# Slot sums kept in SBUF, eight turning PSUM banks, and one row load of a unit cut into 24 and 8 rows, in an attention and soft-MoE kernel on one core

## The chip, the core and the metric

The kernel runs on one core of a Trainium2 chip. The metric is the device time of one execution in microseconds (us). Executions of one kernel lie within a few per cent of each other (the kernel before: 180.0 to 186.27 us over all batches, 3.5%). A run that is over 1.5% above the fastest run of the same kernel counts as "slow". A profile comes from one execution, so a single figure from one profile carries the noise of one run.

## The reference

The kernel computes attention with 8 heads over 8 batches of 576 tokens, and feeds the result to a soft mixture of experts.

```python
# q, k, v: (8 batches, 8 heads, 576 tokens, 64), float32
scores = (q @ k.transpose(0, 1, 3, 2)) / 8
# heads 0-3: the last 32 tokens; heads 4-7: every 4th of the last 128
scores = where(mask[head], scores, -1e6)
x = softmax(scores) @ v                      # -> (4608 tokens, 512)

logits = x @ phi                             # (4608, 32): 8 experts x 4 slots
d = softmax over tokens(logits)
slot_input = d.T @ x                         # (32, 512): the "slot sums"
slot_out[e] = relu(slot_input[e] @ w1[e]) @ w2[e]   # w1: 512x1024, w2: 1024x512
out = softmax over slots(logits) @ slot_out  # (4608, 512)
```

## The kernel before

A Python scheduler places every operation on the five engines before the kernel is built: each operation has a key and a modelled length, and PSUM banks and SBUF rings come from pools. A different pool or key therefore moves instructions on every engine.

The work is cut into eight units (two batches of one head type). Three staging buffers hold the inputs of three units. All loads are issued by one queue, in a fixed order: u0, u1, u2, w10, u3, w11, u4, w12, u5, w13, u6, w14, u7, w15, w16, w17, p3a, p0, p1, p2, p3b. The names w1x are halves of the experts' first layers, p0 to p3b are parts of the second layers. A unit's q, k and v go to 32 partitions each, weights go to 128 partitions, and all are cast from float32 to bfloat16 on the way (the page before has 61.93 MB read from HBM and 30.94 MB on the load queue).

```python
def load_unit(u):
    bp, ty, s = u // 2, u % 2, u % 3
    def f(g):
        for t, src in enumerate((q, k, v)):
            dst = stg[32 * t:32 * t + 32, s, :]
            two = src[2 * bp:2 * bp + 2]
            if ty == 0:
                ...                                   # two loads of 18 KB rows
            else:                                     # one load: 32 rows of 36 KB
                g.dma_start(dst, two[:, 4:8].rearrange("b h (p c) d -> (h p) b (c d)", c=2 * CT))
```

The kernel uses eight PSUM banks. Bank 7 holds the slot sums for the whole kernel, and the other seven turn:

```python
psA  = ps[:, 7, :]
psum = Pool(7, {1: [[6]] + one[:6], 2: [[0, 1], [2, 3], [4, 5]]})
...
i_ = t.matmul(psA[32 * g:32 * g + 32, 256 * ty:256 * ty + 256], et, xb,
              start=b == 0 and i < 4, stop=b == B - 1)         # slot sums, batch b
```

The tail runs after the last batch: slot sums, first layer, then the second layer's matmuls in the order in which its weights arrive (p3a, p0, p1, p2, p3b). The row sum of the output's softmax ("rsum", 36 matmuls) is placed after p1's matmuls. so_sb is the scaled second-layer output; from it the 9.4 MB of output are computed and stored.

```python
PARTS = [("p3a", 3, 0, 8), ("p0", 0, 0, 16), ("p1", 1, 0, 16), ("p2", 2, 0, 16), ("p3b", 3, 8, 16)]
...                            # per part and half: matmuls that need that part's weights
op("pe", rsum, r=b_expT + [b_rowm], w=[rs], alloc=[rs], cost=1.5, key=K1 + 3, after=[mid])
```

The scheduler also has fillers: matmuls whose result nobody reads. They are put where its model leaves a gap of over 0.4 us on TensorE, inside a window FILL of model time. They are meant to keep TensorE's clock up; every kernel here has some of them, so no run shows whether they do.

```python
FILL = (125, 148)
if e == "pe" and fill[0] < t0 and free[e] < fill[1]:
    gap = t0 - max(free[e], fill[0])
    n = min(int((gap - 0.15) / 0.216), 64)
    ...                                             # n filler matmuls, 128x512 each
```

The softmax here doesn't subtract the row's maximum and nothing guards it: scores larger than these inputs give would overflow.

## Time and profile before

The kernel took 181.75 us (median of 3 runs, 180.95 to 182.5).

| what | before |
|---|---|
| span of the profiled execution | 178.9 us |
| load queue (q0), share of all 16 DMA engines' span | 82.9% |
| last weight load, p3b: its sixteen parts land | 147.60 to 151.81 us |
| row sum ends | 151.98 us |
| so_sb starts | 153.24 us |

The landings are the times of the sixteen increments that the load's semaphore gets. I read each as the part of one of the sixteen DMA engines. These come from the trace's semaphore records.

First the page of the kernel before: PEclk is the granted TensorE clock in tenths of full speed and GB/s the load and store rate, each in 40 slices of the span; the last line is a DMA queue with its packets, megabytes and share.

```profile
span 178.9 us, 5741 instructions
...
PEclk9999999999699999999999999999999999999655
...
GB/s 77 198 235 224 187 214 210 228 223 198 221 208 212 243 216 194 213 212 214 236 202 211 214 214 218 233 216 209 227 216 209 216 196 68 78 420 439 469 469 235
...
q0 software_dynamic: 3600, 30.94, 82.9%
```

Counting slices from 0, loads run at some 215 GB/s without a break until slice 32, and before the output the clock is down in slice 10 only. Next the chain that ended last, for the same kernel: start in us, length in us, what ran. "issue" is time in which TensorE (PE) waited for nothing that the profile shows. L849 is the row sum, L834 the second layer's matmuls.

```profile
42.31 1.82 issue
...
64.04 1.05 issue
...
77.21 1.12 issue
...
102.97 1.08 issue
...
150.01 1.97 PE ps L849 x36
151.98 1.24 PE ps L834 x40
153.24 0.49 DVE so_sb L860
```

The row sum ends just after p3b has landed, matmuls of p2 and p3b follow in 1.24 us, and so_sb can start. The loads and the compute chain end together.

### The profile page before, as it was taken

How to read it: one execution, taken by the hardware profiler on the slowest of the kernel's cores; microseconds unless marked ns; L12 is line 12 of the kernel's file. 1: busy time of each engine (PE TensorE's matmuls, PEld its weight loads, DVE VectorE, ACT ScalarE, POOL GpSimd, SP SyncE). 2: the span in 40 equal slices, each digit the busy share in tenths (PEclk: the TensorE clock that was granted, in tenths of full speed). 3: DMA queues.
4: the chain of work that ended last, by engine and by line, in shares of the span. 5: the costliest groups of instructions: out<-in, count | busy, mean ns of one | idle time of the engine just before them, and what ended most of it. 6: DMA issues, size and time to landing. Idle time of an engine off the chain costs nothing.

```text
span 178.9 us, 5741 instructions
## 1 busy us (share of the span) xinstructions
PE 131.7 (74%) x2602; PEld 99.8 (56%) x2602; DVE 116.6 (65%) x262; ACT 92.1 (52%) x132; POOL 27.8 (16%) x56
## 2 busy tenths in 40 slices
PE   0019768885997977978898879788699999889000
PEld 0019557674775955756886757586565569432000
DVE  6980596994279569668859947969974020799200
ACT  2005957843574886568589557477331100599000
POOL 7960402500400250230020010010200000000000
PEclk9999999999699999999999999999999999999655
DMA  5999899999999999999999999999999993299995
GB/s 77 198 235 224 187 214 210 228 223 198 221 208 212 243 216 194 213 212 214 236 202 211 214 214 218 233 216 209 227 216 209 216 196 68 78 420 439 469 469 235
DMA packets 5015, 40.79 MB, mean 228 GB/s; under 512 B 1408, under 2 KB 1408, under 8 KB 1792
## 3 DMA queue, kind: packets, MB, share of 16 engines
q0 software_dynamic: 3600, 30.94, 82.9%
q1 hardware_dynamic: 1392, 9.50, 12.7%
q8 instruction: 20, 0.33, 0.7%
q14 instruction: 3, 0.02, 0.0%
HBM read 61.93 MB, written 9.44 MB: 399 GB/s over the span
## 4 chain that ended last, share of the span: by engine, by line
PE 44%; DVE 32%; ACT 6%; DMA 5%; issue 5%; POOL 1%; DVEq 0%; POOLq 0%
DVE XB L634 9%; DVE PT L584 9%; PE ps L532 7%; PE ps L678 5%; DVE WD L907 5%; DVE VN L599 5%; DMA stg<-in_v_dram 5%; PE ps L651 4%; PE ps L527 4%; PE ps L594 4%; PE ps L924 3%; ACT PT L576 3%; PE ps L569 3%; PE ps L623 2%; PE ps L787 2%
## 5 line engine op out<-in xcount | busy, mean ns | idle before, releaser
L551 ACT ACTIVATE TT<-ps 128x864 f32<-128x864 f32 x32 | 28.6, 896 | 32.9 <-PE ps L532 24.0
L576 ACT ACTIVATE PT<-ps 128x768 bf16<-128x768 f32 x48 | 36.7, 812 | 8.9 <-PE ps L569 8.8
L532 PE MATMUL ps<-ident,stg 96*64 96x96 bf16 x576 | 18.0, 224 | 18.3 <-DMA stg<-in_v_dram 12.8
L634 DVE TENSOR_TENSOR XB<-ps,RV 96x768 bf16<-96x768 f32 x32 | 30.3, 947 | 0.6
L532 PEld LDWEIGHTS ps<-ident,stg 96*64 96x64 bf16 x576 | 15.7, 123 | 20.0 <-DMA stg<-in_v_dram 12.8
L599 DVE COPY VN<-ps 128x768 bf16<-128x768 bf16 x32 | 17.5, 546 | 8.8 <-PE ps L594 8.6
L663 DVE COPY XT<-ps 128x576 bf16<-128x576 bf16 x19 | 11.4, 598 | 13.3 <-PE ps L651 13.2
L623 PE MATMUL ps<-VN,PT 128*128 128x65 bf16 x384 | 17.6, 194 | 1.9 <-DVE PT L584 0.9
L569 PE MATMUL ps<-TT 64*128 64x96 bf16 x384 | 15.1, 204 | 4.2 <-issue 1.1
L594 PE MATMUL ps<-ident,TT 128*128 128x128 bf16 x192 | 16.1, 221 | 1.6 <-issue 1.0
L623 PEld LDWEIGHTS ps<-VN,PT 128*128 128x128 bf16 x384 | 14.4, 98 | 4.0 <-DVE PT L584 1.3
L651 PE MATMUL ps<-ident,XB 96*128 96x96 bf16 x192 | 13.1, 209 | 4.4 <-DVE XB L634 4.3
L527 PE MATMUL ps<-ident,stg 96*128 96x96 bf16 x288 | 14.9, 206 | 0.1
L569 PEld LDWEIGHTS ps<-TT 64*128 64x128 bf16 x384 | 9.5, 94 | 7.9 <-ACT PT L576 1.4
L594 PEld LDWEIGHTS ps<-ident,TT 128*128 128x128 bf16 x192 | 10.9, 98 | 5.4 <-issue 2.4
L651 PEld LDWEIGHTS ps<-ident,XB 96*128 96x128 bf16 x192 | 9.8, 99 | 7.0 <-DVE XB L634 6.0
L584 DVE TENSOR_TENSOR PT<-PT,mask_d 128x768 bf16<-128x768 bf16 x24 | 12.9, 546 | 0.5 <-ACT PT L576 0.2
L527 PEld LDWEIGHTS ps<-ident,stg 96*128 96x128 bf16 x288 | 13.0, 98 | 0.3 <-ACT PT L576 0.3
L584 DVE TENSOR_TENSOR PT<-PT,mask_p 128x768 bf16<-128x768 bf16 x24 | 12.6, 538 | 0.0
L894 PE MATMUL ps<-so_sb,expT 128*128 128x512 bf16 x35 | 10.4, 397 | 0.7 <-DVE stg L907 0.2
L664 ACT ACTIVATE XT<-ps 128x576 bf16<-128x576 bf16 x13 | 8.4, 650 | 3.8 <-PE ps L651 3.5
L678 PE MATMUL ps<-XT,phi_pad 128*128 128x192 bf16 (+1 forms) x64 | 10.2, 306 | 0.2 <-ACT XT L664 0.2
(83 smaller groups left out, 162.6 us busy)
## 6 DMA issues: line engine op xcount, KB each, us to landing
WD<-in_moe_w_dram POOLq DMA_DIRECT2D x7, 1024.0 KB, 27.5
stg<-in_moe_w_dram POOLq DMA_DIRECT2D x2, 2048.0 KB, 19.1
out_dram<-WD SPq DMA_DIRECT2D x1, 4096.0 KB, 11.9
stg<-in_q_dram POOLq DMA_DIRECT2D x8, 288.0 KB, 14.9
stg<-in_k_dram POOLq DMA_DIRECT2D x8, 288.0 KB, 16.7
stg<-in_v_dram POOLq DMA_DIRECT2D x8, 288.0 KB, 18.7
stg<-in_q_dram POOLq DMA_DIRECT2D x4, 576.0 KB, 17.9
stg<-in_k_dram POOLq DMA_DIRECT2D x4, 576.0 KB, 19.8
```

The source lines that it names most:

```text
L527: i_ = t.transpose(bankb2(pt, a)[:, 96 * kk:96 * kk + 96], two[:, c, :], ident[0:96, 0:96])
L532: i_ = t.transpose(bankb2(pt, a)[64 * hx:64 * hx + 64, 96 * kk:96 * kk + 96], src[:, hx, c, :], ident[0:96, 0:96])
L551: return ac.activation(d, sv, ACTF.Copy)
L569: i_ = t.matmul(pair(sc)[:, hx, QB * x:QB * x + QB], win(u, 1, h01, blk_, bpar)[64 * hx:64 * hx + 64], win(u, 0, h01, blk_, bpar)[64 * hx: ...
L576: op("act", lambda ac: ac.activation(sbt(pt)[:, 0:768].rearrange("p (x n) -> p x n", x=2), pair(sc)[:, :, 0:384], ACTF.Exp, scale=SCALE), ...
L584: return dv.tensor_tensor(p_, p_, m.unsqueeze(1).to_broadcast([128, 2, 384]), AluOp.mult)
L594: i_ = t.transpose(bankb(pv)[:, 128 * m:128 * m + 128], win(u, 2, h01, m, bpar), ident[:, :])
L599: op("dve", lambda dv: dv.tensor_copy(sbt(vn)[:, :, :, 0:64], bankb(pv)[:, 0:768].rearrange("p (m x d) -> p m x d", m=6, x=2)), r=[pv], w= ...
L623: i_ = t.matmul(pair(po)[:, bk, 65 * po_:65 * po_ + 65], sbt(pts[i])[:, o_:o_ + 128], sbt(vn)[:, m, half, 0:65], start=True, stop=True)
L634: op("dve", lambda dv: dv.tensor_tensor(sbt(xb)[:].rearrange("p m (x h d) -> p h x m d", x=2, h=2)[:, h01], pv()[:, :, :, 0:64], sbt(rv)[: ...
L651: i_ = t.transpose(bankb(px)[:, QB * m:QB * m + QB], sbt(xb)[:, m, 128 * x:128 * x + 128], ident[0:QB, 0:QB])
L678: i_ = t.matmul(o_, phi_pad[:, c].rearrange("p j i -> p (j i)"), rhs, start=c == 0, stop=c == 3)
```

## The change

The intent: give the eighth PSUM bank to the turning pool, by adding the slot sums of two batches at a time into SBUF; let the scheduler make a tighter order with the new pool; even out the sixteen DMA engines by cutting one load; and start the fillers earlier.

```diff
-FILL = (125, 148)
+FILL = (116, 148)
...
+    scr = sb("scr", [8, 64])
...
-    psA = ps[:, 7, :]
-    one = [[i] for i in range(7)]
-    psum = Pool(7, {1: [[6]] + one[:6], 2: [[0, 1], [2, 3], [4, 5]]})
+    psum = Pool(8, {1: [[i] for i in (6, 7, 0, 1, 2, 3, 4, 5)], 2: [[0, 1], [2, 3], [4, 5], [6, 7]]})
...
-    PACE = 13.1
+    SKEW = 5
+    PACE = 10.87
...                                                  # load_unit, 36 KB rows
-                    res.append(g.dma_start(
-                        dst, two[:, 4:8].rearrange("b h (p c) d -> (h p) b (c d)", c=2 * CT)))
+                    rows = two[:, 4:8].rearrange("b h (p c) d -> (h p) b (c d)", c=2 * CT)
+                    if (u, t) != (SKEW, 0):
+                        res.append(g.dma_start(dst, rows))
+                        continue
+                    res.append(g.dma_start(dst[0:24], rows[0:12]))
+                    res.append(g.dma_start(scr[0:8, :], rows[12:16, :, 0:64]))
+                    res.append(g.dma_start(dst[24:32], rows[12:16]))
...                                                  # seven lines of keys, like this one
-           key=due(u, 0.5 * j))
+           key=due(u, 0.57 * j))
...                                                  # slot sums
-                i_ = t.matmul(psA[32 * g:32 * g + 32, 256 * ty:256 * ty + 256],
+                i_ = t.matmul(bank(acc)[32 * g:32 * g + 32, 256 * ty:256 * ty + 256],
...
+        if b == 1:
+            op("dve", lambda dv: dv.tensor_copy(psA_sb[:], bank(acc)), r=[acc], w=[b_psA], ...)
+        elif b % 2:
+            op("dve", lambda dv: dv.tensor_tensor(psA_sb[:], bank(acc), psA_sb[:], AluOp.add), ...)
...
-    op("dve", lambda vv: vv.tensor_copy(psA_sb[:], psA), r=[b_acc], w=[b_psA], cost=0.65, key=K1)
```

The split concerns one of the 24 q, k and v loads, that of q in unit 5. The tiny load of 1 KB goes to a place that nobody reads. With the new order the scheduler puts 33 fillers between the row sum and p2's matmuls and 8 more before p3b's. The order before has none there. I call these 41 the late fillers.

More of the change, by code (lines that the diff above doesn't have):

```diff
@@ L192, in schedule @@
                 got, tal, ok, taken = [], 0.0, True, {}
+                if any(t.phys is None and t not in o.alloc for t in o.touch):
+                    continue
                 for t in o.alloc:
@@ L378, in bass_dilated_sliding_attn__then__soft_moe_slots_kernel @@
     b_id0, b_id, b_sel, b_fold, b_rowm, b_phist, b_phi = [Buf() for _ in range(7)]
-    b_acc, b_psA, b_csum, b_rcs, b_rtok = [Buf() for _ in range(5)]
+    b_psA, b_csum, b_rcs, b_rtok = [Buf() for _ in range(4)]
     b_expT, b_expX = [Buf() for _ in range(B)], Buf()
@@ L402, in f @@
                 else:
-                    res.append(g.dma_start(
-                        dst, two[:, 4:8].rearrange("b h (p c) d -> (h p) b (c d)", c=2 * CT)))
+                    rows = two[:, 4:8].rearrange("b h (p c) d -> (h p) b (c d)", c=2 * CT)
+                    if (u, t) != (SKEW, 0):
+                        res.append(g.dma_start(dst, rows))
+                        continue
+                    res.append(g.dma_start(dst[0:24], rows[0:12]))
+                    res.append(g.dma_start(scr[0:8, :], rows[12:16, :, 0:64]))
+                    res.append(g.dma_start(dst[24:32], rows[12:16]))
             return res
@@ L503, in bass_dilated_sliding_attn__then__soft_moe_slots_kernel @@
     U = [dict() for _ in range(NU)]
-    XB, XT, ET = {}, {}, {}
+    XB, XT, ET, ACC = {}, {}, {}, {}
     def win(u, t, h01, i, bpar):
@@ L552, in st_T @@
         op("act", ev, r=[pt], **{"w" if j == 0 else "a": [b_TT[u % 2]]}, cost=0.8,
-           key=due(u, 0.8 + 0.5 * j))
+           key=due(u, 0.8 + 0.57 * j))
     def bankb2(t, a):
@@ L573, in pe @@
             return i_
-        k0 = due(u, 4.0 + 1.3 * i)
-        op("pe", pe, r=[b_TT[u % 2]], w=[sc], alloc=[sc, pt], cost=0.22, mode="r", key=k0)
+        k0 = due(u, 5.2 + 1.13 * i)
+        op("pe", pe, r=[b_TT[u % 2]], w=[sc], alloc=[sc, pt], cost=0.28, mode="r", key=k0)
         op("act", lambda ac: ac.activation(
@@ L596, in pe @@
             return i_
-        k0 = due(u, 4.5 + 2.0 * g)
+        k0 = due(u, 3.6 + 2.0 * g)
         op("pe", pe, r=[b_id, b_TT[u % 2]], w=[pv], alloc=[pv, vn], cost=0.35, key=k0)
@@ L626, in pe @@
             return i_
-        k0 = due(u, 8.5 + 2.0 * g)
+        k0 = due(u, 6.7 + 2.46 * g)
         op("pe", pe, r=list(pts.values()) + [vn], w=[po], alloc=al, cost=0.46, key=k0)
@@ L653, in pe @@
             return i_
-        k0 = due(u, 13.0 + 4.0 * bpar + 0.8 * x)
+        k0 = due(u, 19.2 + 4.0 * bpar + 0.1 * x)
         op("pe", pe, r=[b_id, xb], w=[px], alloc=al, cost=0.31, key=k0)
@@ L680, in pe @@
             return i_
-        k0 = due(u, 15.5 + 4.0 * (b % 2))
+        k0 = due(u, 17.4 + 4.0 * (b % 2))
         op("pe", pe, r=[x0, x1, b_phi], w=[lg], alloc=[lg], cost=1.0, key=k0)
@@ L716, in st_L @@
         xb0, xb1 = XB[b, 0], XB[b, 1]
+        if b % 2 == 0:
+            ACC[b // 2] = tile(psum, 1)
+        acc = ACC[b // 2]
         def pe3(t):
@@ L721, in pe3 @@
                 g = (m + 2 * ty) % 4
-                i_ = t.matmul(psA[32 * g:32 * g + 32, 256 * ty:256 * ty + 256],
+                i_ = t.matmul(bank(acc)[32 * g:32 * g + 32, 256 * ty:256 * ty + 256],
                               sbt(et)[:, i, :], sbt((xb0, xb1)[ty])[:, m, :],
-                              start=b == 0 and i < 4, stop=b == B - 1,
+                              start=b % 2 == 0 and i < 4, stop=b % 2 == 1 and i % 6 >= 2,
                               skip_group_check=True)
             return i_
-        op("pe", pe3, r=[et, xb0, xb1], a=[b_acc], cost=0.35, mode="c", key=k0 + 4.0)
+        op("pe", pe3, r=[et, xb0, xb1], after=list(acc.ready), a=[acc],
+           alloc=[acc] if b % 2 == 0 else [], cost=0.44, mode="c", key=k0 + 4.0)
+        if b == 1:
+            op("dve", lambda dv: dv.tensor_copy(psA_sb[:], bank(acc)), r=[acc], w=[b_psA],
+               cost=0.6, key=k0 + 4.6)
+        elif b % 2:
+            op("dve", lambda dv: dv.tensor_tensor(psA_sb[:], bank(acc), psA_sb[:], AluOp.add),
+               r=[acc], w=[b_psA], cost=0.6, key=k0 + 4.6)
     W_AFTER = {2: ["w10"], 3: ["w11"], 4: ["w12"], 5: ["w13"], 6: ["w14"],
```

## The prediction

> **What bounds the kernel now.** The DMA bounds the first 150 of 178.9 us: in the page's slices it stays at 9 tenths; the load queue takes 82.9% of all 16 engines' span. The loads are issued in one order and never starve. In the semaphore records of the last weight load, p3b, the sixteen engines' parts land between 147.6 and 151.8 us: eight engines by 148.9, the other eight from 150.1. The compute chain has been tuned to end with it: in the timeline the row-sum matmuls (L849) end at 151.98, 48 small matmuls follow (L834), so_sb starts at 153.24, and from there 25 us of output (9.4 MB) follow, which the change doesn't touch. Both must move: the last load, and the row sum.
>
> **What the change does.**
> 1. An eighth PSUM bank turns (four pairs, not three), against four adds or copies of about 0.69 us on DVE (the length of the old copy, L763), off the end.
> 2. A new order. Replaying both instruction orders with the median length of each operation in this trace, without stalls, I estimate that the row sum ends 6.4 us earlier (139.4 for 145.8).
> 3. The split row load. [...] If the right four are relieved, the slowest engine gains up to 1.2 us; the mean of the last landings is 149.4, so never over 2.4. The least sure step.
> 4. Fillers. The changed order has 33 filler matmuls before p2's matmuls and 8 before p3b's, the old one none. They run, early or late: 41 x 0.216 us = 8.9 us (three took 0.81). They cost nothing only if the row sum ends by about 142.
>
> **Is it early enough?** The trace's row sum ends 6.2 us later than my stall-free replay of the same kernel. The timeline shows why: PE stands still for no visible cause ("issue") at 42.3, 64.0, 71.4, 77.2 and 103 us for 0.5 to 1.8 us, each ending some 1.4 us after a 16 KB packet of the instruction queue; after the longest the granted clock is 0.5 for 3.4 us. [...] A faster PE runs into this more. With like stalls I estimate the row sum at 144 to 147, the fillers then end after p3b has landed, and so_sb starts at 154 to 157: later than now. With few stalls it starts at 151 to 152.4.
>
> **Prediction.** 183.8 us, 179.6 to 188.0 eight times in ten. Faster by over 2% 0.05 (the load floor forbids it), within 2% 0.57, slower by over 2% 0.38.
>
> **What would show it.** Right: row sum ends before 148; the 33 fillers end after p2 (146) and delay p3b's matmuls past its landing; instruction-queue packets ahead of PE gaps; last output still 25 us after so_sb. Wrong: the fillers end before the loads, the chain of waits shows DMA into TT, p3b's slowest part lands near 150.5; then about 180. Slower still if stalls of over 1.5 us bring the half clock twice.

In point 3, that the split relieves four of the sixteen engines is my assumption, and the 1.2 us are my estimate from it: no record of these traces names the engine of a packet.

## The result, and the profile after

The changed kernel took 196.45 us (median of 4 runs, 194.96 to 199.07), against 181.65 us (180.95 to 182.5, 4 runs) for the kernel before on the same chip. The ratio is 1.0785 with a 95% interval of 1.0701 to 1.087: slower. A ratio here is the mean time of one kernel's fast runs over that of the other's fast runs of the same rounds, so it is not quite the ratio of the medians. The time lies far above the predicted range.

| what | before | after |
|---|---|---|
| span of the profiled execution | 178.9 us | 193.3 us |
| p3b: first, mean and last of sixteen landings | 147.60, 149.33, 151.81 | 151.52, 155.82, 157.99 |
| row sum ends | 151.98 | 157.28 |
| late fillers end | none | 167.25 |
| so_sb starts | 153.24 | 167.64 |

The page after, with the same lines as before:

```profile
span 193.3 us, 5830 instructions
...
PEclk9999999988999969999985699995799999999755
...
GB/s 88 208 221 230 189 215 234 212 199 218 213 212 238 179 150 176 187 189 189 190 193 167 214 217 219 222 217 217 217 217 212 185 58 2 0 328 452 414 434 326
...
q0 software_dynamic: 3696, 30.94, 80.8%
```

The same 30.94 MB are loaded, but the rate is down from slice 13 to slice 21 (about 63 to 106 us), to 150 GB/s at the lowest. The clock is down in several stretches and not in one. At the end of the loads there is a hole: slices 33 and 34 move 2 and 0 GB/s, so almost nothing was loaded or stored for some 10 us. The chain that ended last, after (L865 is the row sum, L940 a filler, L850 the second layer):

```profile
38.52 2.93 issue
...
65.68 2.74 issue
...
81.75 1.44 issue
...
89.43 1.44 issue
...
96.53 1.76 issue
...
103.92 2.58 issue
...
155.32 1.97 PE ps L865 x36
...
157.36 7.07 PE ps L940 x32
164.43 0.99 PE ps L850 x32
...
165.58 1.67 PE ps L940 x7
167.25 0.36 PE ps L850 x8
167.64 0.49 DVE so_sb L876
```

Two things are to be seen. The stretches of "issue" are longer: the six shown add up to 12.9 us, the four longest of before to 5.1 us. And the tail has fillers in it: TensorE runs 7.07 us of fillers after the row sum, then p2's matmuls, then 1.67 us of fillers, then p3b's, which had landed at 157.99, long before. The output part has not changed: so_sb starts 14.40 us later, and the span is 14.4 us longer.

The third view is the table of windows: us, busy time with instruction counts of PE, PEld, DVE, ACT and POOL, granted clock, DMA share and GB/s. First before, then after.

```profile
70.00:80.00 10.00, 7.84 (x172) 6.42 (x170) 7.26 (x16) 6.02 (x9) 2.61 (x5) 1.00 1.04 216
...
100.00:110.00 10.00, 8.57 (x186) 6.78 (x188) 6.85 (x15) 5.76 (x11) 0.53 (x1) 1.00 1.03 215
```

```profile
70.00:80.00 10.00, 9.02 (x175) 7.40 (x171) 6.71 (x16) 7.46 (x12) 2.61 (x5) 0.88 1.05 166
...
100.00:110.00 10.00, 6.47 (x116) 5.88 (x116) 2.91 (x5) 3.95 (x6) 0.53 (x1) 0.50 1.01 188
```

From 70 to 80 us, TensorE does about the same number of matmuls, but the DMA moves 166 GB/s for 216, while its share of busy time is the same or higher (1.05 for 1.04). So the engines are not starved of requests; they take longer for each byte. From 100 to 110 us the load rate is still down, and TensorE, at half clock, does 116 matmuls for 186.

The packets' durations say the same. In the second table, "long" is the share of load packets in a stretch of 3 us that took over 5% more than the usual time of their size (for instance 1378 ns for 18 KB and 625 ns for 8 KB).

```
packets of 18,432 B, us       median   nine in ten below
before, 60 to 110 us          1.378    1.378
after, 60 to 85 us            1.378    1.983
after, 85 to 110 us           1.525    1.880

after, at us                  60     63     69    75    81     90    99     from 105 on
share of long packets         0.03   0.55   1.0   1.0   0.19   1.0   0.78   0.01
```

### The profile page after: what moved, and what is told of

It is laid out like the page before. It is cut to its first block, busy times and chain, and to the rows that moved or that the text cites. A ratio compares the mean times of both kernels' runs of the same rounds, so it can differ in the third digit from the quotient of the medians.

```text
span 193.3 us, 5830 instructions
## 1 busy us (share of the span) xinstructions
PE 144.0 (74%) x2635; PEld 109.3 (57%) x2642; DVE 111.0 (57%) x253; ACT 97.9 (51%) x144; POOL 29.0 (15%) x58
## 3 DMA queue, kind: packets, MB, share of 16 engines
q0 software_dynamic: 3696, 30.94, 80.8%
## 4 chain that ended last, share of the span: by engine, by line
PE 53%; DVE 13%; ACT 12%; issue 9%; DMA 5%; POOL 1%; DVEq 0%; POOLq 0%
PE ps L539 10%; PE ps L940 7%; ACT PT L583 7%; PE ps L534 6%; PE ps L685 5%; PE ps L630 5%; DVE WD L923 5%; DMA stg<-in_v_dram 5%; PE ps L601 4%; PE ps L658 3%; PE ps L576 3%; DVE XB L641 2%; PE ps L850 2%; DVE PT L591 2%; PE ps L803 2%
## 5 line engine op out<-in xcount | busy, mean ns | idle before, releaser
L539 PE MATMUL ps<-ident,stg 96*64 96x96 bf16 x576 | 18.9, 238 | 21.3 <-DMA stg<-in_v_dram 12.7
L539 PEld LDWEIGHTS ps<-ident,stg 96*64 96x64 bf16 x576 | 17.5, 134 | 22.3 <-DMA stg<-in_v_dram 12.7
L671 ACT ACTIVATE XT<-ps 128x576 bf16<-128x576 bf16 x25 | 15.8, 661 | 9.1 <-PE ps L658 9.1
L601 PE MATMUL ps<-ident,TT 128*128 128x128 bf16 x192 | 17.6, 231 | 1.1 <-ACT TT L558 1.0
L639 DVE RECIPROCAL RV<-ps 96x12 f32<-96x12 f32 x32 | 7.0, 220 | 19.9 <-PE ps L630 19.7
L576 PE MATMUL ps<-TT 64*128 64x96 bf16 x384 | 16.1, 207 | 1.6 <-ACT expT L690 1.0
L534 PE MATMUL ps<-ident,stg 96*128 96x96 bf16 x288 | 14.8, 206 | 1.4 <-issue 1.4
L940 PE MATMUL ps<-mask_p,ident 128*128 128x512 bf16 x59 | 14.8, 388 | 0.8 <-issue 0.7
L658 PE MATMUL ps<-ident,XB 96*128 96x96 bf16 x192 | 14.8, 229 | 0.3 <-DVE XB L641 0.3
L601 PEld LDWEIGHTS ps<-ident,TT 128*128 128x128 bf16 x192 | 12.2, 104 | 3.5 <-ACT TT L558 1.4
L658 PEld LDWEIGHTS ps<-ident,XB 96*128 96x128 bf16 x192 | 11.7, 112 | 1.1 <-DVE XB L641 0.4
```

Of the source, the lines that this page charges most:

```text
L534: i_ = t.transpose(bankb2(pt, a)[:, 96 * kk:96 * kk + 96], two[:, c, :], ident[0:96, 0:96])
L539: i_ = t.transpose(bankb2(pt, a)[64 * hx:64 * hx + 64, 96 * kk:96 * kk + 96], src[:, hx, c, :], ident[0:96, 0:96])
L576: i_ = t.matmul(pair(sc)[:, hx, QB * x:QB * x + QB], win(u, 1, h01, blk_, bpar)[64 * hx:64 * hx + 64], win(u, 0, h01, blk_, bpar)[64 * hx: ...
L601: i_ = t.transpose(bankb(pv)[:, 128 * m:128 * m + 128], win(u, 2, h01, m, bpar), ident[:, :])
L658: i_ = t.transpose(bankb(px)[:, QB * m:QB * m + QB], sbt(xb)[:, m, 128 * x:128 * x + 128], ident[0:QB, 0:QB])
L940: i_ = te.matmul(bank(t)[:, 0:512], ident[:, :], mask[0][:].rearrange("p m x -> p (m x)")[:, 0:512], start=True, stop=True)
```

## The experiments

My first theory was this. The split slows the loads; later loads, and with them a later fetch of instructions, make the row sum late; a late row sum exposes the fillers. The rival: the new order by itself makes TensorE stall more, so that the row sum would be late, and the fillers exposed, without the split too. Eleven runs were made, of ten kernels (a_neither was run twice), in three batches, each batch with its own runs of the kernel before on the same chip. The texts give what each theory, and variants of them, expected.

### The split undone: a_nosplit

```diff
-                    if (u, t) != (SKEW, 0):
+                    if True:
```

> The changed kernel with the unit-5 q row load left whole (32 rows, no tiny load); every instruction on PE, DVE, ACT and SP is in the same place. Theory A (the split load slows the packets that follow, 18,432 B packets 1.38 to 1.9 us between 64 and 108 us, and so both the weights and the instruction blocks come late): packets stay at 1.38 us, the last weight load lands at about 151 to 152 instead of 158.0, the row sum ends at 144 to 149 instead of 157.3, the fillers then hold the PE until 153 to 158, and the time is 183 to 188. Theory B (the new order and the eight banks disturb the loads by themselves, the split is harmless): packets still stretch after 64 us, the last load lands at 156 or later, the time stays above 192.

Measured: 191.39 us (190.9 to 192.17), ratio to before 1.0552 (1.0486 to 1.0618). p3b lands from 147.49 to 151.23 us, as before the change, and the stretch of the packets is gone. The row sum ends at 152.10, as in the kernel before. The chain that ended last:

```profile
150.14 1.97 PE ps L865 x36
152.18 7.07 PE ps L940 x32
159.25 0.99 PE ps L850 x32
...
160.40 1.67 PE ps L940 x7
...
162.46 0.49 DVE so_sb L876
```

Undoing the split gives back 5.1 us. But all of p2 and p3b had landed by 151.23 here, and the fillers still ran until 162.07. So they need no late load to cost their full length: they cost it because the row sum ends at 152, as it did in the kernel before. The kernel is slower than the first theory expected.

### The late fillers taken out: a_nolatefill

```diff
-FILL = (116, 148)
+FILL = (116, 137)
```

The 33 and the 8 fillers go, and everything else keeps its place on every engine.

> The changed kernel, split kept, without the 33 and the 8 filler matmuls after the row sum (the filler window ends earlier; nothing else moves). Theory A: row sum still ends at about 157 and the last load lands at about 158, but so_sb starts at about 158.8 instead of 167.6, so the time falls by 8 to 9 us to 187 to 188. Rival: the fillers only filled a wait, and the time falls by less than 2 us.

Measured: 184.71 us (183.44 to 188.11), ratio 1.0157 (1.0076 to 1.0237). p3b lands from 149.21 to 155.50, the row sum ends at 154.98 and so_sb starts at 156.24. The late fillers cost 11.7 us by the medians (196.45 less 184.71), more than their length of some 9 us. Row sum to so_sb fell from 10.36 to 1.26 us, which is 9.1 us. The expectation had the row sum at about 157 and the time at 187 to 188; both came lower. The rest, some 2 us, comes with a row sum that ended earlier, though TensorE's instructions are the same up to there; a_nosplit against a_neither shows the same (152.10 and 150.61). I don't know the reason. It may be scatter: these are single profiles, and the second profile of a_neither's kernel (a_neither_again, a slow run) has its row sum at 154.29.

### Both undone: a_neither

Both edits together leave the new order, the eight banks and the earlier start of the fillers. No run tells these three apart.

> The changed kernel without the split and without the late fillers: the new order and the eight banks alone. Theory A: last load lands at 151 to 152, the row sum ends at 144 to 149, before the load; so_sb starts at about 152.4; time 180 to 181.5, that is 0.5 to 1.5 us below the kernel before. Theory B: above 186.

Measured: 179.88 us (179.61 to 182.18), ratio 0.9953 (0.9856 to 1.005): the same as before within 2%, and not told apart from 1. Its chain at the end:

```profile
148.64 1.97 PE ps L865 x36
150.61 1.24 PE ps L850 x40
151.87 0.49 DVE so_sb L876
```

The row sum ends at 150.61, 1.4 us earlier than before and not 6.4, and later than the 144 to 149 of the expectation. The runs of these kernels make a square (medians in us):

```
                     whole load            split load         cost of the split
no late fillers      179.88 (a_neither)    184.71             4.8
late fillers         191.39 (a_nosplit)    196.45 (after)     5.1
cost of the fillers   11.5                  11.7
```

These are medians of all runs, and "after" was timed in an earlier batch. By the means of the fast runs alone the split costs 3.9 and 4.5 us, the fillers 11.1 and 11.7. The two costs add up and do not need each other. The chain "split, so late row sum, so exposed fillers" is not what happens: the fillers cost as much without the split.

### The split alone on the kernel before: b_split

The edit adds the split's lines of the change, and scr, to the kernel before.

> The kernel before with the split row load alone (same unit, same rows, same tiny load). Theory A: packets stretch after the split for tens of us, landings of the sixteen engines spread to 6 us or more, the last load lands near 157 to 158 and the time is 187 to 190. Theory B: nothing changes by more than 1 us, time 181 to 182.5.

Measured: 185.28 us (184.65 to 187.09), ratio 1.0228 (1.0148 to 1.0307), 4.1 us over the kernel before of the same rounds (181.22). p3b lands from 150.64 to 156.55, with a mean of 153.83. The harm is there, but smaller than the 187 to 190 us expected. So the split costs 4 to 5 us with either order and with either set of banks.

### Which part of the split: b_split_notiny and b_tiny_only

```diff
# b_split_notiny: the split, less this line
-                    res.append(g.dma_start(scr[0:8, :], rows[12:16, :, 0:64]))
# b_tiny_only: the whole load, then the tiny one
+                    res.append(g.dma_start(dst, rows))
+                    res.append(g.dma_start(scr[0:8, :], rows[12:16, :, 0:64]))
```

> The kernel before with the unit-5 q load split in 24 and 8 rows, without the tiny load between. If the harm of the split comes from the imbalance that the tiny load causes ([...]engines work in loads of different shape at once), [...]nothing is out of step, packets stay at 1.38 and 0.63 us, the last load lands at 151 to 152, time 181 to 182.5. If splitting by itself is the harm[...], the packets stretch as in b_split and the time is 184 to 186.

> The kernel before with the q load whole and the tiny load of 8 short rows after it. Imbalance theory: nothing out of step, no stretch, time 181 to 182.5. Rival (the tiny load itself, or a lasting shift of the engines that later loads get, is the harm): stretch after 62 us, time 184 to 186.

Measured: 181.72 us (ratio 1.0036, 0.9907 to 1.0166) without the tiny load, and 181.79 us (1.0047, 0.9866 to 1.0228) with the tiny load alone. p3b's last part lands at 151.50 and 151.90, and no packets are stretched. The windows from 70 to 80 us, of b_split, then of b_split_notiny, then of b_tiny_only (last column GB/s):

```profile
70.00:80.00 10.00, 7.28 (x155) 5.90 (x159) 6.16 (x13) 5.12 (x8) 2.61 (x5) 0.99 1.06 175
```

```profile
70.00:80.00 10.00, 8.77 (x188) 6.85 (x185) 7.46 (x16) 6.61 (x11) 2.61 (x5) 1.00 1.02 213
```

```profile
70.00:80.00 10.00, 8.78 (x179) 6.72 (x172) 7.31 (x17) 7.33 (x12) 2.61 (x5) 1.00 1.03 214
```

Neither part does harm alone (181.72 and 181.79 us, for 185.28 with both). It takes 24 rows, a tiny load, and then 8 rows. No record of these traces names the engine of a packet, so it is not shown which engines the rows went to. What the runs show is that of these three only the order 24, tiny, 8 makes the sixteen landings this uneven: those of w13, the next weight load, spread over 72.90 to 80.36 us after the change (71.78 to 79.53 in b_split) for 72.84 to 74.69 before (72.69 to 74.47 in b_split_notiny).

The two parts of the cost can be told apart by a sum. If a row takes the same time wherever it goes (before, from 60 to 110 us, a packet of 18 KB took 1.378 us both at the median and at nine in ten), moving rows from some engines to others leaves the mean of the sixteen landings where it was. But the mean landing of p3b went from 149.33 before to 155.82 after, 6.5 us later, and in b_split to 153.83, 4.5 us later; even the first of them came later (151.52 and 150.64 for 147.60). So, if each landing is one engine's, most of the loss is not the extra rows of some engines: it is that the packets of all were longer for a while (at 69 and 75 us after the change, every load packet was a long one).

### The split in a later unit: b_split_u7

```diff
-    SKEW = 5
+    SKEW = 7
```

This goes into the kernel of b_split. Unit 7 is the last unit; after it, only weights are loaded.

> The kernel before with the split and the tiny load in unit 7, the last unit, in place of unit 5. If packets stretch only where lagging engines are still in a unit's 32-row loads while others are in a 128-row weight load (or the other way round), only one such border is left after unit 7, so stretch is confined to some 10 us after 90 us, and the loads end 1 to 2.5 us late (153 to 154.5), time 182 to 184.5. If every packet after the split is slowed for some 45 us, whatever its shape, the weight loads stretch to 130 us and the time is again 185 or more.

Measured: 183.05 us (181.14 to 185.45), ratio of fast runs 1.0048 (0.9914 to 1.0181). The profiled run was a slow one, so I use only its loads. The windows from 90 to 110 us:

```profile
90.00:100.00 10.00, 8.39 (x202) 7.03 (x199) 6.07 (x12) 7.94 (x12) 1.05 (x2) 1.00 0.94 167
100.00:110.00 10.00, 7.11 (x180) 5.84 (x182) 6.78 (x13) 4.68 (x7) 0.53 (x1) 1.00 1.03 215
```

Packets are stretched between 87 and 99 us (up to 0.9 of them are long). From 99 us on, at most 3 in 100 are, although the parts of the next load land 6.2 us apart (103.13 to 109.35), about as unevenly as after the change. p3b's last part lands at 153.06, 1.3 us later than before and not 4 to 6. So uneven landings alone do not stretch packets. In this kernel and in the changed one packets were long where a unit's load (32 partitions) and a weight load (128 partitions) followed each other, and not where whole weight loads did. After the change the landings of such neighbours overlap: w13's from 72.90 to 80.36 us and u6's from 74.65 on, w14's from 88.04 to 96.17 and u7's from 91.62 on. Before it they hardly do (w13's end at 74.69, u6's start at 74.24; w14's end at 88.81, u7's start at 88.90). Why packets are longer there is not shown.

### Where TensorE stands still: a_neither_shift

The new order alone, with 64 small matmuls first on TensorE. Nothing else moves on any engine. By a block I mean what one packet of 16 KB of the instruction queue brings, as I read the trace: before the change there are 20 such packets for 5204 matmuls and weight loads, which gives an estimate of 260 to a packet.

```diff
+    def dummy(t):
+        for _ in range(64):
+            i_ = t.matmul(bank(dm)[0:32, 0:32], ident[:, 0:32], ident[:, 0:32],
+                          start=True, stop=True)
+        return i_
+    op("pe", dummy, r=[b_id], w=[dm], alloc=[dm], cost=2.0, key=-1)
```

> a_neither with 64 short dummy matmuls (32 columns, about 2 us) put first on PE, where it waits for the first load anyway: 128 PE instructions more, half a 256-instruction block, all else in the same order on all engines. If the PE gaps of a_neither (3.6 us at 41, 2.0 at 69, 2.7 at 100) are late instruction blocks, they sit at fixed instruction counts, and all three move to other matmuls, about half a block earlier or later: I expect the longest gap near 41 us to fall from 3.6 to under 2, split over two places. If the gaps belong to what the matmuls there wait for (data, banks, a busy port), they stay at the same matmuls, at 41, 69 and 100 us, with the same lengths. Time within 1% of a_neither either way, since the last load ends at 151.3.

Measured: 182.6 us (181.72 to 183.09), ratio 1.0104 (1.0022 to 1.0187). The timeline of TensorE, first of a_neither, then of a_neither_shift; the columns are start in us, length, engine, line, operation, tile, count, and in brackets the idle time before it with its releaser:

```profile
36.41 1.55 PE L539 MATMUL ps<-ident,stg 96*64 96x96 bf16 x64
41.44 0.53 PE L539 MATMUL ps<-ident,stg 96*64 96x96 bf16 x8 [3.48 <-issue]
```

```profile
36.27 0.23 PE L547 MATMUL ps<-ident,stg 96*64 96x96 bf16 x1
39.84 3.09 PE L547 MATMUL ps<-ident,stg 96*64 96x96 bf16 x71 [3.33 <-issue]
```

The same group of 72 transposes is torn in both: after its 64th matmul in one, after its first in the other, and both times that is the 605th matmul that the trace has, counted from the start of the program by the weight loads. (By the places it is 63 matmuls and not 64; a record can be missing from a trace.) The other long gaps behave alike (gaps in this table and the next are between one weight load and the next, so they come out up to 0.1 us longer than between matmuls):

```
matmuls done before the gap  605    1113   1241   1749   1877
a_neither, gap in us         3.58   2.00   0.93   2.73   -
a_neither_shift              3.46   -      3.15   1.89   0.96
after                        3.03   2.84   0.96   3.50   -
before, near these counts    1.92   -      1.23   1.22   -
(- is no gap over 0.85 us)
```

The counts are 128 (1113 to 1241, 1749 to 1877), or nearly four times 128 (508), apart. A gap that keeps its count, and not its place in the work, comes from the instructions themselves and not from data or banks. Each of these gaps in a_neither and a_neither_shift ends 1.2 to 1.6 us after a packet of 16 KB of the instruction queue has landed. 128 matmuls with their 128 weight loads are 256 instructions, close to the estimate of 260 to a packet. The theory of instruction blocks holds for these gaps; the expected figure for the longest gap (under 2 us) does not.

The traces also show which blocks stall. Between the 350th and the 1880th matmul, the eleven profiles of fast runs hold 132 blocks. Ahead of the 51 gaps of over 0.85 us, the packet starts a median of 4.1 us after TensorE has entered the block before, takes some 1 us, and TensorE goes on 1.2 to 1.8 us after its landing. From entry to going on that is 5.6 to 8.2 us, with a median of 6.6. A block that TensorE is through sooner than that ends in a gap. Of the 39 blocks that it finished in under 5.3 us, 37 were followed by a gap of over 0.85 us; of the 31 that took 6.7 us or more, none was followed by one of over 0.23. The blocks that end at counts 605 and 1749 take 3.2 and 3.3 us in a_neither (gaps 3.58 and 2.73), those that end at 605 and 1753 take 4.9 and 5.2 us before the change (1.92 and 1.22). a_neither_shift bears this out: its shift gives the block that ends at 1113 more work (5.65 us for 4.15) and the gap there falls from 2.00 to 0.23, while the block that ends at 1241 has less (3.14 us for 5.26) and the gap grows from 0.93 to 3.15. The start also scatters from run to run: for the block that ends at 605 it came 3.2 us after entry in b_tiny_only and 4.2 us before the change, with the same instructions (gaps 0.82 and 1.92).

What the gaps cost can be read from two kernels with one order. b_tiny_only and before have the same instructions on TensorE. In the profiled runs, the gaps over 0.85 us between 25 and 131 us add up to 4.1 and 8.7 us, the time at half clock is 3.4 us in both, and the last slot sums end at 132.6 and 137.1 us. The 4.7 us of gaps are the 4.5 us by which TensorE is later. b_split_notiny, with the same instructions too, lies between (7.9 and 136.5). The earlier row sum of b_tiny_only brings no time, because TensorE then waits for p3b's last part (L855 is the row sum, L840 the second layer):

```profile
145.45 2.04 PE L855 MATMUL ps<-rowm,expT 128*128 128x1 bf16 x36
...
151.94 1.04 PE L840 MATMUL ps<-TT,hT 128*32 128x256 bf16 x16 [3.46 <-DMA TT<-in_moe_w_dram]
```

The sums of all kernels, one profiled run each:

```
                 gaps, us   half clock, us   slot sums end   row sum ends
b_tiny_only       4.1        3.4              132.6           147.50
before            8.7        3.4              137.1           151.98
b_split          10.1       13.7              141.8           156.72
a_neither        11.4       17.1              135.1           150.61
a_nosplit        11.7       16.1              136.6           152.10
a_nolatefill     16.8       14.4              139.4           154.98
after            16.4       17.6              141.7           157.28
```

The new order has more of both than the old (a_neither against before), and the split adds about 5 us of gaps to the new order and 1.4 us to the old. In the stretch of slow load packets, the instruction packets were slow too (1.31 to 1.62 us each between 65 and 105 us after, 0.89 to 1.31 before), and so even blocks of 5.5 to 6.6 us stalled there (counts 1241 to 1621 after, gaps 0.96 to 1.90).

### Looking for a better version: a_neither_again, c_balA, c_balB

If the tiny load can make the landings uneven (w13's 7.5 us apart for 1.9), it might also even them out. p2 is followed by p3b, weights after weights, where b_split_u7 had shown no stretch (at most 3 in 100 packets were long). Both versions are made from a_neither, and p2's 128 rows are cut:

```diff
# c_balA: 112 rows, 8 rows, tiny, 8 rows
+        parts = [(dst[0:112], src[0:112]), (dst[112:120], src[112:120]), (scr[0:8], ...), (dst[120:128], src[120:128])]
# c_balB: 112 rows, tiny, 8 rows, tiny, 8 rows
+        parts = [(dst[0:112], src[0:112]), (scr[0:8], ...), (dst[112:120], src[112:120]), (scr2[0:8], ...), (dst[120:128], src[120:128])]
```

> The same kernel as a_neither, as the measure for the two below on the same chip and to tell 0.5% from nothing: new order and eight banks alone, 0.990 to 1.000 of the kernel before.

> a_neither, with the second last weight load (p2, 128 rows) cut in 112 rows, 8 rows, a tiny load of 8 short rows, 8 rows: after all unit loads, so that only weight loads follow. [...] No stretch in any case, as nothing of another shape follows. If the 8 are the earlier engines, the parts of the last load p3b land within about 2.5 us and end near 150.2 instead of 151.3, time 0.5% below a_neither; if they are the later ones, they end near 152.4, 0.6% above.

> The same with a tiny load ahead of each of the two groups of 8 rows[...]: the sign opposite to c_balA, one of the two ending near 150.2 and the other near 152.4.[...]

Both texts rest on my assumption that each group of 8 rows goes to eight of the engines, and that a tiny load changes which eight; no record of these traces names the engine of a packet.

Measured, in 5 rounds: a_neither_again 183.63 us over all six runs (179.83 to 184.85, four of them slow), ratio of fast runs 0.9968 (0.9871 to 1.0065); c_balA 181.09 us, 1.0012 (0.9948 to 1.0076); c_balB 182.5 us, 1.0077 (1.0018 to 1.0136), so slower by under 2%. p3b's last part lands at 152.77 and 153.83, later than in a_neither (151.25) in both, where I expected one to be earlier. And packets were stretched here too: from 110 to 150 us one in ten of the 8 KB packets took 975 and 832 ns or more, for 625 ns. So my rule from b_split_u7, that weights after weights are safe, does not hold for a load cut this way. No version beats both kernels beyond doubt: a_neither is the best, and in two batches its interval includes 1.

## Why the prediction was wrong

The change costs 14.8 us by the medians. The parts measured are 11 to 12 us for the late fillers, 4 to 5 us for the split, and a gain of some 1.3 us for the order, the banks and the earlier fillers, which is not told apart from nothing.

- **The load floor and the output part: right.** The loads bound the kernel before: b_tiny_only's row sum ended 4.5 us earlier, at 147.50, and its time was the same (181.79 us). The output takes as long after so_sb as it did.
- **The split, "the slowest engine gains up to 1.2 us": wrong in sign.** The step rested on an assumed count of rows per engine, which no trace shows, and was put down as the least sure one. p3b's last part came 6.2 us later after the change, 4.7 us later with the split alone. The landings did become uneven, but their mean rose by 4.5 to 6.5 us, which rows moved at an unchanged 1.378 us each would not do: packets became longer, all of them at 69 and 75 us, and the longest tenth took 1.983 us and more for 1.378, that is 1.44 times.
- **The row sum, "With like stalls I estimate the row sum at 144 to 147": the term that was mis-sized.** It came at 157.28, and at 150.61 with neither split nor late fillers. The stall-free replay said 139.4 for the new order and 145.8 for the old, a gain of 6.4 us; the gain measured is 1.4. "Like stalls" was the error: the mechanism (packets of the instruction queue, then half clock) was named, but it was taken to cost what it had cost before. It did not, because a stall is what is left of some 6 to 7 us (measured: 5.6 to 8.2, median 6.6) after the block's own run time, and the new order runs through some blocks in 3.2 us. Gaps went from 8.7 to 11.4 us by the new order and to 16.4 with the split, and half clock from 3.4 to 17 us. The prediction had said that a faster TensorE "runs into this more", and gave it no number.
- **The fillers, "They cost nothing only if the row sum ends by about 142": right, and it was the larger part of the loss.** Their length of 8.9 us was right too (7.07 and 1.67 us in the chain, with two records missing). What was wrong is the share that shows: with so_sb at 154 to 157, the prediction left some of them hidden behind the loads. With the row sum at 152 or later, nothing is left to hide behind, as a_nosplit shows with all loads landed at 151.23.
- **The signs named beforehand.** The fillers ended after p2 and held up p3b's matmuls, with instruction packets ahead of the gaps, as said under "Right"; "row sum ends before 148" failed. "Slower still if stalls of over 1.5 us bring the half clock twice" is what came: it came in four spells by 131 us, at 41.7, 69.0, 99.7 and 130.4.

What stays open: why packets are longer where loads of different shapes overlap; why the instruction packet starts only some 4 us after a block is entered; what the new order, the eight banks and the earlier fillers do each by itself; and some 2 us of the fillers' cost that lies ahead of them.

## What to carry to other kernels

Filler matmuls placed by a model are real work on the chip (here 8.7 us in the chain, at a cost of 11 to 12 us): put them where a wait is certain in the profile, never between a late chain and the end of the kernel, and set their window by measured times. A replay without stalls overstates what a tighter order brings, because the stalls belong to the order too: here 37 of the 39 blocks of some 128 matmuls that were done in under 5.3 us were followed by one. Price a new order by the run time of each of its blocks, not with the stalls of the old one. Before work is moved between DMA engines, check that the mean of the landings stays where it was: here it rose from 149.33 to 155.82 us as the rate fell to 166 GB/s for 216 (70 to 80 us), and evening out could have won 2.5 us at most (the last landing before, 151.81, less the mean).

## What the traces show of instruction blocks, the clock and the loads

- With the DMA busy at 9 tenths or more, the crossings from one instruction block to the next show as TensorE gaps of 0.9 to 4.1 us (4.13 in c_balA), which end 1.2 to 1.8 us after the block's packet lands, where TensorE ran through the block before in well under 6 us (37 of the 39 blocks done in under 5.3 us); in b_tiny_only and before they set TensorE's end (4.7 us of gaps, 4.5 us of time).
- Up to 135 us, the half-clock records are multiples of 3.413 us long and start on a grid of 3.413 us (41.68, 68.99 and 99.71 after the change). A single gap much shorter than such a window was followed by half clock: 1.92 us before the change (it ended at 44.1, the half clock began at 44.3), and 1.89 us after it (it ended at 98.3; half clock from 99.7 for 10.24 us). In the eleven fast profiles, from 20 to 135 us, every full-clock window of this grid with TensorE busy for at most 0.56 of it (25 of them) was followed by half clock, and none with over 0.63 was.
- Where landings of loads to 32 and to 128 partitions overlapped after the change, an 18 KB packet took up to 1.98 us (nine in ten below, 60 to 85 us) for 1.38, and the rate fell to 166 GB/s for 216 (70 to 80 us).
- A 1 KB load between the two parts of a cut load went with a loss of 3.6 us by the medians: b_split took 185.28 us, b_split_notiny 181.72.
